# One-row gate matmul widened to 128 rows, and the order of work laid out anew, in a fused attention and gated-MLP kernel

## The chip, the cores and the metric

The kernel runs on one core of a Trainium2 chip. The metric is device time in microseconds (us). Five engines matter here: TensorE (PE in the profile; its weight loads are listed apart as PEld), VectorE (DVE), ScalarE (ACT), GpSimd (POOL), and SyncE (SP), which issues most of the DMAs. Each engine works through its own list of instructions in order, and the engines wait for one another on semaphores.

## The reference

`x` is 2048 tokens of 512 features, in bfloat16. A gate value per token, `g = sigmoid(sum(x * gate_w))`, mixes two branches:

```
g = sigmoid((x * gate_w).sum(-1, keepdims=True))
a = attention(x)             # 32 heads of 16, four segments of 512 tokens
b = ((relu(x @ W_gate)) * (x @ W_up)) @ W_down      # 512 -> 1792 -> 512
return g * a + (1 - g) * b
```

The attention branch takes the tokens in four segments. Inside a segment it is causal softmax attention over 512 tokens per head. Over segments it keeps a memory: `M` and `z` collect the keys (through an elu-like map `phi`) and values of earlier segments, and `num / den` reads them with the queries. The two parts are mixed per head by `sigmoid(beta)`, and a final projection by `wo` follows.

For this case the row `gate_w` matters: 512 numbers in DRAM that every one of the 128 partitions needs as a copy, since the sum over features is taken by VectorE with tokens on partitions.

## The kernel before

**Stages.** All weights are loaded once and stay on the chip. For each segment `s` of 512 tokens there are:

- `proj(s)` (lines 774 to 818): query, key and value projections, 4 x 3 tiles of four 128x512 matmuls (lines 786 and 788).
- `att(s)` (lines 876 to 1023): 18 "visits" of the score matrix. One visit is a block of small matmuls on 32 rows each (line 908, "quad"), which fills four PSUM banks, and one `Exp` by ScalarE over 128x2048 (line 924), which empties them. The next quad writes the same four banks, so it waits for that `Exp`. GpSimd masks the diagonal blocks (line 930). After the visits of a head group comes the product with the values ("pv", line 964, matmuls on 64 rows and 17 columns): 16 in all, followed by VectorE transposes and a scaling.
- `mu(s)` and `nd(s)` (lines 823 to 864): update and read of the memory; `mu` runs as matmuls on 32 columns (line 831), three times in all.
- `ffn(s)` (lines 1028 to 1050): 14 x 2 tiles of four matmuls (line 1038), evacuated by ScalarE or VectorE as relu (lines 1046 and 1047) and by VectorE as a product (line 1049).
- `outp(s)` (lines 1052 to 1093): the output projection and `W_down` into one PSUM bank (lines 1070 and 1077), scaled (lines 1086 and 1087) and stored.

**What sets the order.** The order of instructions on each engine isn't written by hand. Every piece of work is an `Op` with an assumed duration, its reads and writes, and a place in one of several queues per engine with a priority. While the program is built, `Sched.run` (line 486) plays a list scheduler: `ready` (line 308) says when an op could start, `_choose` (line 443) takes the best head of the queues, and `place` (line 364) appends it to the engine's program with the waits that it needs and moves the engine's planned clock on. Equal choices are broken by a random number (`jitter`, line 436) whose seed changes with every 8 us of TensorE's planned time (`knob`, line 428; `WIN`, line 35); the same seed also draws small changes of the priorities. The list of seeds stands at line 546. TensorE's planned clock gets `SWITCH` (line 28) added whenever the op's mode differs from that of the op before (line 392): "f" is a matmul on the full array, "r" a quad, "h" a pv, "c" a `mu`. So a change to one assumed duration, to `SWITCH` or to the seeds changes which op is taken next from that point on, on all engines.

**The gate row.** In the first microseconds ScalarE's queue issues two small DMAs: a 1 KB read into `adT` that is read by nobody (`touch`, line 602) and `gate_w` into row 0 of the tile `oTt` (line 603). The other 127 rows of `oTt` hold whatever they held. SP meanwhile issues the tokens of segment 0 into `hT` (line 604) and the weights. GpSimd builds the identity matrix and masks (lines 646 to 658). TensorE runs five warm-up matmuls, transposes `hT` against the identity (line 683), a second small warm-up (line 699), begins the query projection, and then runs the matmul named `gwx`:

```
lhsT = ones[0:1, 0:128], rhs = oTt[0:1, 0:512]  ->  PSUM bank 2, 128 x 512
```

It has one row of contraction, so each of the 128 output partitions gets one times `gate_w`. ScalarE copies the bank to `gwb` (line 706, `gwc`), and VectorE uses `gwb` in the gate sums (lines 734 and 742). `gwx` may not be planned before 6.4 us (line 705). Later `oTt` serves as scratch for VectorE's transposes (line 992).

Of the kernel before, what the change touches and what calls it, by code (L numbers as in the profile page):

```python
# [11 lines left out]
BF16 = mybir.dt.bfloat16  # L12
# [12 lines left out]
TNN = 4  # L25
STRICT = 6000.0
PE_LAT = 175.0
SWITCH = 100.0
GATE_T = {1: 44000.0, 2: 90000.0, 3: 140000.0}
UNIT_T = 400.0  # L30
NBLK = 36
# [91 lines left out]
class Sched:  # L123
# [240 lines left out]
    def place(self, op, e, start):  # L364
# [26 lines left out]
        if e == "pe":  # L391
            if op.mode != self.mode or start > self.now[e] + 60.0:
                occ += SWITCH
            self.mode = op.mode
# [127 lines left out]
def plan(S, D, F):  # L522
    NT, KT, NF = S // 128, D // 128, F // 128
    return [
        ("xT", [128, KT, XR * 512], BF16), ("wq", [128, KT, 512], BF16), ("wk", [128, KT, 512], BF16), ("wv", [128, KT, 512], BF16),
        ("wo", [128, 4, 512], BF16), ("wg", [128, KT, F], BF16), ("wu", [128, KT, F], BF16), ("wd", [128, NF - SBX, 512], BF16),
        ("qT", [128, QTN, 512], BF16), ("kT", [128, 4, 512], BF16), ("kp", [128, 5, 8, 128], BF16),
        ("phiq", [128, 4, 512], BF16), ("ek", [128, EKN, 512], BF16), ("phik", [128, 4, 512], BF16), ("ttmp", [128, 2, 512], BF16),
        ("vaug", [128, 2, 4, 32, 17], BF16), ("vsh", [128, 4, 32, 17], BF16), ("E", [128, NBLK * 512], BF16),
        ("Tn", [128, TNN, 512], F32), ("adT", [128, 512], BF16), ("oTt", [128, 512], BF16),  # L530
        ("amem", [128, 2, 512], BF16), ("amemT", [128, 4, 512], BF16), ("oT", [128, OTN, 512], BF16),
        ("hT", [128, HTN, 512], BF16), ("rl", [128, 3, 512], BF16), ("osb", [128, 3, 512], BF16),
        ("Mc", [128, 4, 34], F32), ("Mbd16", [128, 4, 136], BF16), ("mumask", [128, 4, 136], F32),
        ("braw", [128, 32], BF16), ("eb", [128, 32], F32), ("romgh", [128, 32], F32), ("epsv", [128, 32], F32),
        ("gexp", [128, NT], F32), ("omg", [128, NT], F32), ("gexpT", [128, NT * 4], F32), ("gwb", [128, 512], BF16),  ("gl", [128, NT], F32),
        ("rden", [128, 64], F32), ("rdg", [128, 64], F32), ("rdm", [128, 128], F32), ("pm8", [128, 8], F32), ("pm", [128, 2], F32), ("ident", [128, 128], BF16),
    ]


def build_kernel(nc, A_x, A_wq, A_wk, A_wv, A_wo, A_beta, W_g, W_u, W_d, gate_w, out):  # L540
    _, S, D = A_x.shape
    F = W_g.shape[1]
    assert D == 512 and S % 512 == 0 and F % 128 == 0
    NSEG, KT, NF, NT = S // 512, D // 128, F // 128, S // 128
    EPS, SCALE = 1e-6, 16 ** -0.5
    sc = Sched(seeds=(140892, 575458, 0, 581332, 635069, 619273, 262375, 763595, 0, 238677, 585783, 19046, 187739, 0, 462444, 519459, 197962, 296149, 243870, 832001, 511906, 535245, 636171, 100007, 0, 121574, 418075, 0, 0, 346384, 0,))
    T = {}
    with contextlib.ExitStack() as stack:
        for name, shape, dt in plan(S, D, F):
            T[name] = stack.enter_context(nc.sbuf_tensor(name, shape, dt))  # L550
        PS = stack.enter_context(nc.psum_tensor("ps", [128, 8, 512], F32))
        for st in sc.streams:
            sc.sem[st] = stack.enter_context(nc.semaphore(f"s_{st}"))
        program(sc, nc, T, PS, A_x, A_wq, A_wk, A_wv, A_wo, A_beta, W_g, W_u, W_d, gate_w, out, NSEG, KT, NF, NT, EPS, SCALE)
        with nc.Block() as block:
            sc.emit(block)
    return sc


def program(sc, nc, T, PS, A_x, A_wq, A_wk, A_wv, A_wo, A_beta, W_g, W_u, W_d, gate_w, out, NSEG, KT, NF, NT, EPS, SCALE):  # L560
    V = type("V", (), T)
    PL = PS[:, 0:4, :]
    PF = PS[:, :, :].rearrange("q b n -> q (b n)")

    def op(eng, fn, occ, **k):
        return sc.add(Op([(eng, fn, occ)], **k))

    def pe(fn, occ, **k):
        k.setdefault("lat", PE_LAT)
        if k.get("role") == "w":  # L570
            k["reads"] = list(k.get("reads", ())) + [f"init{i}" for i in range(4)]
        return op("pe", fn, occ, **k)
# [10 lines left out]
    def pool(fn, occ, **k):  # L583
        return op("pool", fn, occ, **k)

    def dma(eng, fn, nbytes, occ=500.0, **k):
        return op(eng, fn, occ, dma=True, nbytes=nbytes, **k)
# [9 lines left out]
    def load(eng, names, dst, src, nbytes, occ=460.0):  # L597
        (lact if eng == "act" else lsp).append(dma(eng, lambda e, dst=dst, src=src: e.dma_start(dst, src), nbytes, occ=occ, writes=names, name="ld" + names[0]))  # L598
    x0 = A_x[0, 0:512, :].rearrange("(i p) d -> p i d", p=128)
    def touch(n, src):  # L600
        load("act", ["adT"], V.adT[0:16, 32 * n:32 * n + 32], src, 1024)
    touch(0, A_wq[0:16, 0:32])
    load("act", ["oTt"], V.oTt[0:1, :], gate_w.rearrange("(a n) -> a n", a=1), 1024)
    for i in range(4):
        load("sp", [f"hT{i}"], V.hT[:, i, :], x0[:, i, :], 1 << 17)
# [40 lines left out]
    st = []  # L646
# [15 lines left out]
        ds.append(dve(lambda e, b=b: e.memset(PS[:, 4 + b, :], 0.0), 500, writes=[f"init{b}"], name=f"init{b}"))  # L662
    ds.append(dve(lambda e: e.reduce_sum(V.pm[:, :], V.pm8[:, :].rearrange("q (j p) -> q p j", p=2), AX.X), 180, reads=["pm8"], writes=["pm"], name="pm"))
    sc.queue(0, ds)
    sc.queue(1, st)

    def warm(m, n, k, b):
        def fn(e):
            for i in range(m):
                ins = e.matmul(PL[:, b, 0:n], lhsT=nc.const_aps.tensor(1.0, [128, 128], BF16), rhs=nc.const_aps.tensor(1.0, [128, n], BF16), start=True, stop=True)  # L670
            return ins
        return pe(fn, m * n * (0.834 if k == 0 else 0.5), writes=[f"bankL{b}"], name=f"warm{k}")

    xps, xcs = [warm(5, 512, 0, 3)], []
# [26 lines left out]
            ins = e.matmul(A(epw)[:, 0:n], lhsT=nc.const_aps.tensor(1.0, [128, 128], BF16), rhs=nc.const_aps.tensor(1.0, [128, n], BF16), start=True, stop=True)  # L701
        return ins
    xps.append(pe(warm1, 380, name="warm1", ep=epw, role="w"))
    xps.append(pe(lambda e: e.matmul(PL[:, 2, :], lhsT=nc.const_aps.tensor(1.0, [128, 128], BF16)[0:1, :], rhs=V.oTt[0:1, :], start=True, stop=True), 300, reads=["oTt"], writes=["bankL2"], name="gwx"))  # L704
    xps[-1].after = 6400.0
    xcs.append(act(lambda e: e.activation(V.gwb[:], PL[:, 2, :], ACT.Copy), t_act(512), reads=["bankL2"], writes=["gwb"], name="gwc"))
    sc.queue(0, xps)
# [458 lines left out]
def bass_gated_mix__memory_aug_infini_attn__glu_gated_reglu__prompt_kernel(  # L1166
    nc, A_x, A_wq, A_wk, A_wv, A_wo, A_beta, B_x, B_W_gate, B_W_up, B_W_down, gate_w, out
):
    return build_kernel(nc, A_x, A_wq, A_wk, A_wv, A_wo, A_beta, B_W_gate, B_W_up, B_W_down, gate_w, out)
# [28 lines left out]
```

## Time and profile before

| what | value |
|---|---|
| time, median of 3 runs (lowest to highest) | 264.85 us (264.82 to 264.95) |
| the profiled execution's own time | 265.14 us |
| its span, first to last instruction | 263.4 us |
| TensorE busy | 255.4 us, 97% of the span |
| ScalarE busy | 184.9 us, 70% |
| VectorE busy | 181.0 us, 69% |
| GpSimd busy | 129.8 us, 49% |
| DMA engines busy, mean of 16 | 87% from 5.88 to 45 us, 6% to 28% in the stretches after |
| granted TensorE clock | 1.00 over the span |

The profiled execution's time is 1.74 us above its span: that is what lies around the first and the last instruction. A line of the timeline has a start, a length, the engine, the source line, the operation, what it writes and reads, the shape and a count of merged instructions. TensorE's matmuls are pipelined, so the recorded length of one (380 ns for 512 columns) is longer than the distance to the next one's start; the cost of a matmul is read from the distances between starts. A letter q behind an engine's name is its DMA queue or its sequencer.

### The profile page before, as it was taken

The page shows a single profiled execution, that of the slowest core. Times are in us where ns is not written, and L with a number is a line of the kernel's source. Part 1 is how long each engine was busy: PE and PEld are TensorE (multiplying, and loading weights), DVE is VectorE, ACT ScalarE, POOL GpSimd, SP SyncE. Part 2 cuts the span into 40 slices and gives each one's busy share as a digit, 9 for nine tenths or more (in the row PEclk, how much of TensorE's full clock was granted, in tenths as well). Part 3 has the DMA queues.
Part 4 walks back from the last instruction along what each step waited for, and adds up shares of the span by engine and source line. Part 5 has one row for each costly group of instructions (what it writes and reads, how often), then busy time and mean ns, then how long its engine had stood idle before and what let it go on. Part 6 is the DMA issues. An engine that isn't in the chain of part 4 may idle for free.

```text
span 263.4 us, 6630 instructions
## 1 busy us (share of the span) xinstructions
PE 255.4 (97%) x2713; PEld 113.6 (43%) x2748; DVE 181.0 (69%) x355; ACT 184.9 (70%) x159; POOL 129.8 (49%) x295
## 2 busy tenths in 40 slices
PE   8999999999999999999999999999999999999996
PEld 4444444444343544434343444444444444444444
DVE  5788788889788555787877765775873857267610
ACT  4577589976788956877778986978765765767021
POOL 3025646564646354774646366776564443535200
PEclk9999999999999999999999999999999999999999
DMA  6899584024250023210273014110032101100011
GB/s 182 235 383 223 85 270 132 4 41 71 56 115 27 3 65 80 63 41 3 58 138 74 20 42 81 41 25 20 20 80 49 22 0 42 41 2 0 2 40 40
DMA packets 34527, 19.22 MB, mean 73 GB/s; under 512 B 24001, under 2 KB 33986, under 8 KB 34498
## 3 DMA queue, kind: packets, MB, share of 16 engines
q1 hardware_dynamic: 34368, 18.80, 29.4%
q8 instruction: 21, 0.34, 0.5%
q14 instruction: 8, 0.07, 0.1%
q10 hardware_dynamic: 130, 0.01, 0.0%
HBM read 9.75 MB, written 2.11 MB: 45 GB/s over the span
## 4 chain that ended last, share of the span: by engine, by line
PE 94%; DMA 2%; issue 2%; SPq 0%; DVE 0%; DVEq 0%
PE ps L1038 36%; PE ps L1077 19%; PE ps L788 11%; PE ps L908 9%; PE ps L964 7%; PE ps L1070 5%; PE ps L786 5%; DMA phik<-ek 1%; PE ps L851 1%; DMA hT<-in_A_x_dram 1%; PE ps L831 1%; SPq L598 0%; PE ps L683 0%; DVE osb L1086 0%; PE ps L704 0%
## 5 line engine op out<-in xcount | busy, mean ns | idle before, releaser
L930 POOL TENSOR_SCALAR_AFFINE_SELECT E<-E 64x256 bf16<-64x256 bf16 (+1 forms) x256 | 108.9, 437 | 110.1 <-ACT E L924 81.3
L924 ACT ACTIVATE E<-ps 128x2048 bf16<-128x2048 f32 x72 | 135.1, 1876 | 36.4 <-PE ps L908 36.0
L1038 PE MATMUL ps<-xT,wu 128*128 128x512 bf16 x214 | 57.5, 380 | 1.4 <-issue 1.3
L1038 PE MATMUL ps<-xT,wg 128*128 128x512 bf16 x217 | 57.7, 380 | 0.8 <-issue 0.6
L1077 PE MATMUL ps<-wd,hT 128*128 128x512 bf16 (+2 forms) x229 | 52.3, 366 | 1.1 <-issue 1.0
L1049 DVE TENSOR_TENSOR hT<-ps,rl 128x512 bf16<-128x512 f32 x56 | 38.2, 682 | 18.8 <-PE ps L1038 18.4
L974 DVE STREAM_TRANSPOSE Tn<-ps 128x512 f32<-128x512 f32 x32 | 21.2, 695 | 17.8 <-PE ps L964 17.7
L1038 PEld LDWEIGHTS ps<-xT,wg 128*128 128x128 bf16 x224 | 20.6, 98 | 25.9 <-issue 3.5
L1077 PEld LDWEIGHTS ps<-wd,hT 128*128 128x128 bf16 x238 | 21.4, 98 | 23.8 <-issue 2.8
L1038 PEld LDWEIGHTS ps<-xT,wu 128*128 128x128 bf16 x224 | 19.9, 98 | 25.7 <-issue 3.2
L908 PE MATMUL ps<-qT,kp 32*128 32x192 bf16 (+7 forms) x512 | 28.6, 287 | 0.0
L1047 DVE TENSOR_SCALAR rl<-ps 128x512 bf16<-128x512 f32 x31 | 21.3, 688 | 5.0 <-PE ps L1038 4.3
L1046 ACT ACTIVATE rl<-ps 128x512 bf16<-128x512 f32 x25 | 14.9, 598 | 12.8 <-PE ps L1038 12.8
L908 PEld LDWEIGHTS ps<-qT,kp 32*128 32x128 bf16 x512 | 8.2, 92 | 25.8 <-issue 14.4
L964 PE MATMUL ps<-E,vaug 64*17 64x128 bf16 (+7 forms) x512 | 18.7, 283 | 0.0
L964 PE MATMUL ps<-E,vsh 64*17 64x128 bf16 (+7 forms) x512 | 18.3, 283 | 0.0
L1087 ACT ACTIVATE osb<-ps,omg 128x512 bf16<-128x512 f32 (+1 forms) x9 | 6.1, 675 | 15.6 <-PE ps L1070 14.4
L1086 DVE TENSOR_SCALAR osb<-ps,omg 128x512 bf16<-128x512 f32 (+1 forms) x8 | 5.6, 700 | 16.3 <-PE ps L1070 10.1
L1070 PE MATMUL ps<-wo,oT 128*128 128x512 bf16 (+2 forms) x68 | 16.5, 367 | 0.0
L788 PE MATMUL ps<-xT,wk 128*128 128x512 bf16 x62 | 16.2, 380 | 0.2 <-issue 0.2
L788 PE MATMUL ps<-xT,wq 128*128 128x512 bf16 x62 | 15.9, 379 | 0.3 <-issue 0.2
L786 PE MATMUL ps<-wv,xT 128*128 128x512 bf16 x59 | 15.1, 380 | 0.7 <-issue 0.6
(74 smaller groups left out, 232.7 us busy)
## 6 DMA issues: line engine op xcount, KB each, us to landing
vsh<-vaug SPq DMA_DIRECT2D x8, 272.0 KB, 3.9
out_dram<-osb SPq DMA_DIRECT2D x15, 128.0 KB, 1.7
wg<-in_B_W_gate_dram SPq DMA_DIRECT2D x8, 224.0 KB, 5.1
wu<-in_B_W_up_dram SPq DMA_DIRECT2D x8, 224.0 KB, 5.3
wd<-in_B_W_down_dram SPq DMA_DIRECT2D x1, 1792.0 KB, 9.1
osb<-in_A_x_dram SPq DMA_DIRECT2D x12, 128.0 KB, 2.3
hT<-in_A_x_dram SPq DMA_DIRECT2D x4, 128.0 KB, 2.3
wq<-in_A_wq_dram SPq DMA_DIRECT2D x4, 128.0 KB, 2.9
```

The lines of the kernel that those rows point to most:

```text
L786: ins = e.matmul(A(ep)[:, :], lhsT=V.xT[:, kt, tok + col * 128:tok + (col + 1) * 128], rhs=w[:, kt, :], start=(kt == 0), stop=(kt == KT - 1))
L788: ins = e.matmul(A(ep)[:, :], lhsT=w[:, kt, col * 128:(col + 1) * 128], rhs=V.xT[:, kt, tok:tok + 512], start=(kt == 0), stop=(kt == KT - 1))
L908: ins = q.matmul(dst, lhsT=V.kp[r, kslot(s, G), c, :], rhs=V.qT[r, qslot(s, G), q0:q0 + w], start=True, stop=True, tile_position=(32 * jj, ...
L924: acts.append(act(lambda a: a.activation(V.E[:, base * 512:base * 512 + min(2048, 4 * W)], PF[:, 0:min(2048, 4 * W)], ACT.Exp, scale=SCALE ...
L930: pools.append(pool(lambda g, ap=ap, lim=lim, pat=pat: g.affine_select(out=ap, in_=ap, compare_op=ALU.is_ge, fill=0.0, base=lim, pattern=[ ...
L964: ins = q.matmul(A(eps[p])[32 * jj:32 * jj + 17, 64 * (c + u):64 * (c + u + n)], lhsT=v[:, 8 * G + 2 * jj + p, :], rhs=V.E[r, f:f + 64 * n ...
L974: ds.append(dve(lambda e, p=p, ep=eps[p]: e.transpose(V.Tn[:, 2 * (G % (TNN // 2)) + p, :], A(ep)[:, :]), t_dve(512), writes=[f"Tn{2 * (G ...
L1038: ins = e.matmul(A(ep)[:, :], lhsT=w[:, kt, f * 128:(f + 1) * 128], rhs=V.xT[:, kt, c % XR * 512:(c % XR + 1) * 512], start=(kt == 0), sto ...
L1047: ("dve", lambda e, ep=eg, r=r: e.tensor_scalar(V.rl[:, r, :], A(ep)[:, :], 0.0, None, ALU.max), t_dve(512))],
L1049: evs.append(dve(lambda e, ep=eu, r=r, hs=hs: e.tensor_tensor(V.hT[:, hs, :], A(ep)[:, :], V.rl[:, r, :], ALU.mult), t_dve(512), reads=[f" ...
L1070: ins = e.matmul(A(ep)[:, 0:c1 - c0], lhsT=V.oT[:, ot[G], i * 128:(i + 1) * 128], rhs=V.wo[:, G, c0:c1], start=st_ and G == 0, stop=sp_ an ...
L1077: ins = e.matmul(A(ep)[:, 0:c1 - c0], lhsT=V.hT[:, slots[f], i * 128:(i + 1) * 128], rhs=V.wd[:, f, c0:c1], start=st_ and f == f0, stop=sp ...
```

## The change

Four lines change, and one is added:

- `gz`, a new GpSimd instruction, sets all of `oTt` (128 x 512, bfloat16) to zero. It is put second in GpSimd's list, between the two instructions that build the identity. Since it writes `oTt`, the DMA of `gate_w` into row 0 now waits for it.
- `gwx` contracts over all 128 rows of `oTt` with a 128x128 matrix of ones, so 127 of the products are zeros. Its assumed duration falls from 300 to 216 ns.
- `SWITCH` rises from 100 to 104 ns.
- The list of seeds is another one, with 29 entries in place of 31.

The computed values are the same. What each engine does in total is the same but for `gz` and the shape of `gwx`; the order in which the scheduler lays it out is drawn anew.

```diff
-SWITCH = 100.0
+SWITCH = 104.0
...
-    sc = Sched(seeds=(140892, 575458, 0, 581332, 635069, 619273, 262375, 763595, 0, 238677, 585783, 19046, 187739, 0, 462444, 519459, 197962, 296149, 243870, 832001, 511906, 535245, 636171, 100007, 0, 121574, 418075, 0, 0, 346384, 0,))
+    sc = Sched(seeds=(249524, 599739, 0, 545337, 139743, 284348, 57498, 932614, 741284, 496270, 730785, 169184, 0, 723979, 219278, 211335, 0, 499970, 629776, 0, 138415, 940641, 908855, 0, 156145, 0, 475937, 427456, 0,))
...
     touch(0, A_wq[0:16, 0:32])
+    gz = pool(lambda e: e.memset(V.oTt[:, :], 0.0), 250, writes=["oTt"], name="gz")
     load("act", ["oTt"], V.oTt[0:1, :], gate_w.rearrange("(a n) -> a n", a=1), 1024)
...
-    sc.queue(1, st)
+    sc.queue(1, [st[0], gz] + st[1:])
...
-    xps.append(pe(lambda e: e.matmul(PL[:, 2, :], lhsT=nc.const_aps.tensor(1.0, [128, 128], BF16)[0:1, :], rhs=V.oTt[0:1, :], start=True, stop=True), 300, reads=["oTt"], writes=["bankL2"], name="gwx"))
+    xps.append(pe(lambda e: e.matmul(PL[:, 2, :], lhsT=nc.const_aps.tensor(1.0, [128, 128], BF16), rhs=V.oTt[:, :], start=True, stop=True), 216, reads=["oTt"], writes=["bankL2"], name="gwx"))
```

## The prediction, made before the result was known

> **What bounds the kernel now.** I read the page first, then the waits, then TensorE's timeline.
>
> ```profile
> span 263.4 us, 6630 instructions
> PE 255.4 (97%) x2713; PEld 113.6 (43%) x2748; DVE 181.0 (69%) x355; ACT 184.9 (70%) x159; POOL 129.8 (49%) x295
> PE 94%; DMA 2%; issue 2%; SPq 0%; DVE 0%; DVEq 0%
> ```
>
> TensorE is busy for 97% and makes 94% of the chain that ended last; no other engine passes 70%. The question is whether the remaining per cents are idle time that another order could fill. TensorE's own waits:
>
> ```profile
> PE ps L1038 <- issue: 1.9, 12, 0.2
> PE ps L1077 <- issue: 1.0, 6, 0.2
> PE ps L670 <- PEq L1183: 0.8, 1, 0.8
> ```
>
> Apart from the start (0.8) nothing is named but "issue", at most 0.2 us each. The timeline tells what these are:
>
> ```profile
> 24.44 1.03 PE L1038 MATMUL ps<-xT,wu 128*128 128x512 bf16 x4
> 25.40 0.40 PE L908 MATMUL ps<-qT,kp 32*128 32x256 bf16 x8
> 25.73 1.04 PE L1038 MATMUL ps<-xT,wg 128*128 128x512 bf16 x4
> 26.60 0.38 PE L1038 MATMUL ps<-xT,wu 128*128 128x512 bf16 x1
> ```
>
> A full 512-column matmul costs 0.216 us (four in a row between 25.73 and 26.60, 0.87). From 24.44 to 25.40 four take 0.96: entering the quad costs 0.10 more. The quad holds TensorE for 0.33. Where 0.16 of "issue" stands, the next start is one whole 0.216 later, and the groups by line hold 217 and 214 matmuls of L1038 where the program has 448: these are missing records, not idle time. The same holds for the chain's "DMA phik<-ek": in its 3.4 us TensorE's timeline runs on at 0.216 a matmul.
>
> I summed TensorE's work from the first projection (5.88) to the end of the last matmul (260.94), with distances between starts. Wide matmuls: 910 of 512 columns at 0.2158 are 196.4; 18 of 384 at 0.163 and 18 of 128 at 0.056 are 3.9; 48 of the memory read at 0.063 are 3.0. Row- or column-tiled blocks: 72 quads at 0.329 are 23.7, 16 pv at 1.10 are 17.6, 3 mu at 0.59 are 1.8. Entries from full-array matmuls into tiled blocks: I count 74 in the timeline (17 of the 91 blocks follow another tiled block and pay none) at 0.102, 7.5. The gate matmul is 0.41. Together 254.3 of 255.1: at most 0.8 us of the whole stretch can be waiting. TensorE's own work is the bound, with hardly any slack to win.
>
> **The change, part by part.**
>
> *The matmul.*
>
> ```profile
> 5.88 1.02 PE L788 MATMUL ps<-xT,wq 128*128 128x512 bf16 x4
> 6.83 0.38 PE L704 MATMUL ps<-oTt,const-bfloat16-1.0 1*128 1x512 bf16 x1
> 7.15 0.60 PE L788 MATMUL ps<-xT,wq 128*128 128x512 bf16 x2
> ```
>
> The four before it should fill 4 x 0.216 = 0.86 but its start is 0.95 after theirs: 0.09 of entry. Its successor comes 0.32 after it: 0.216 and 0.10 of exit. As a full matmul amid full ones it costs 0.216 like its neighbours, so 0.09 + 0.10 = 0.19 to 0.20 goes. Bounds: 0.20 gained, or nothing if the cost hangs on something other than its one row. I take 0.20, because every full-to-full step around it shows 0.216 and every full-to-tiled one shows the extra.
>
> Here a rule speaks against the change. The Trainium skill's page "TensorE: Matmul & The Clock Gate", section "LDWEIGHTS (loading the stationary operand)", says that a weight load's time goes by its columns and not by the contraction length; its section "Why this matters for your kernels" adds that a single matmul with 32 rows takes as long as one with 128. By that rule the gain is 0 and the time 264.85; by the row above it is 0.20. The trace agrees on the weight load alone, 90 ns with one row against 98 with 128, and not on the distances to the neighbours. The Trainium skill's page "TensorEngine Tiling (Array Packing)", section "Key Properties", has that case: a change of tiling mode drains TensorE.
>
> What is late next if this 0.20 goes: the weights. The four issues of wu end near 12.6 with a median of 5.3 to landing, the last near 17.5; their first reader starts at 18.39. With everything 0.20 sooner 0.7 is left.
>
> *The memset and the later DMA.*
>
> ```profile
> 0.80 0.20 POOL L647 MEMSET ident<- 128x128 bf16 x1 [0.29 <-POOLq L1183]
> 1.08 0.29 POOL L648 TENSOR_SCALAR_AFFINE_SELECT ident<-ident 128x128 bf16<-128x128 bf16 x1
> 1.24 0.54 ACTq L598 DMA_DIRECT2D oTt<-in_gate_w_dram  x1
> 1.81 1.28 ACT L695 ACT_TABLE_LOAD   x1 [1.81 <-issue]
> 2.92 0.37 PEld L683 LDWEIGHTS ps<-ident,hT 128*128 128x128 bf16 x4 [0.70 <-DMA hT<-in_A_x_dram]
> 4.13 1.03 ACT L695 ACTIVATE xT<-ps 128x512 bf16<-128x512 f32 x2 [1.04 <-PE ps L683]
> ```
>
> GpSimd's memset of 512 columns isn't in the trace. From below: 0.20, the memset of 128 columns; from above: four of these, 0.80. Between the 8-column memset (0.10) and the 128-column one (0.20) the slope gives 0.10 + 504 x 0.00083 = 0.52, an estimate from these rows, which I take. Behind it on GpSimd: the identity would be ready near 1.9 (2.2 by the upper bound) in place of 1.37; its reader at 2.92 waits for the tokens' DMA. VectorE's reduction of the mask (3.01) and GpSimd's own next work (15.32) have more room. Cost 0; past 1.5 us of memset it would push the transposes.
>
> The wait stands in ScalarE's queue: the gate DMA goes out near 1.6 (1.9 at most) in place of 1.24, and behind it the table load moves to about 2.2 (2.5) and ends by 3.4 (3.8), before its user at 4.13. SP's queue isn't behind it. The DMA has no landing row; ScalarE's other 1 KB reads land after 1.9 to 4.8, so it is there by about 3.5 (6.7 at the extreme) for a reader at 6.83. Cost 0. If that cover went, the price would be the lateness itself, since the projection stands behind the gate matmul on TensorE.
>
> *The order.* TensorE's instructions are the same set, so the order moves time in two ways only: the number of entries into tiled blocks, and waits. One entry is 0.10. The scheduler takes a pv next to a quad where it can (11 pv run straight into a quad, 3 follow one), so I expect 74 plus or minus 3 entries, 0.3 us, and take 0 for the mean. The four-nanosecond rise of `SWITCH` costs nothing itself; it moves the plan's clock.
>
> Waits can only be added. Their nearest row is the exponential that empties a quad's banks:
>
> ```profile
> 20.23 1.88 ACT L924 ACTIVATE E<-ps 128x2048 bf16<-128x2048 f32 x1 [1.48 <-PE ps L908]
> 22.37 0.40 PE L908 MATMUL ps<-qT,kp 32*128 32x320 bf16 x8
> 22.48 0.60 ACT L1046 ACTIVATE rl<-ps 128x512 bf16<-128x512 f32 x1 [0.37 <-PE ps L1038]
> ```
>
> It ends at 22.11 and the quad starts at 22.37: 0.26 later. Over the quads that distance is 0.26 at the least, in seven of them, and 0.70 in the median, and no quad was late. Bounds of the new waits: 0 as now, and from above these seven each behind one more evacuation of 0.60, 7 x (0.60 - 0.26) = 2.4. I take 0, nearest to the order seen, in which every quad kept the distance. The moved DMA issues sit on SP, which no row shows as a bound.
>
> The tail stays: the last evacuation (0.35) and store follow the last matmul in any order.
>
> **Sum.** Profiled execution: 265.14 (263.4 of span and 1.74 around it) - 0.20 + 0 + 0 = 264.94. It stood 0.29 above the median, so the median goes from 264.85 to 264.65, -0.08%. Within 0.2%, 0.53 us, a measurement of this kernel can hardly tell it from no change.
>
> **Rivals.**
>
> *Fewer entries.* The new draw puts more pv and quads side by side. It is past 0.2% from four entries fewer: -0.20 - 4 x 0.10 = -0.60, 264.25; six give 264.05. For it: 74 entries for 91 blocks leave room, as no pv has a quad on both sides. Against it: 14 of 16 pv already have one quad neighbour, and of idle time there is at most 0.8 us to win.
>
> *Quads behind a late exponential.* Slower than before. The new order puts an evacuation of 0.60 ahead of the exponential on ScalarE, where its quad has the 0.26 only: TensorE, in order, waits 0.34. It decides from three such visits (1.0 less the 0.20 gained is 0.8, over 0.53). With one a segment it is 4 x 0.34 = 1.36: 266.0. For it: the relu sits right beside the exponential on ScalarE (22.48), and seven visits have only the 0.26. Against it: ScalarE is at 70%, and this scheduler kept the distance in every visit.
>
> *The full matmul saves nothing.* The extra at 6.83 would come from what TensorE does there and not from the one row: 264.85. For it: the weight load of one row (90 ns) is as long as one of 128 (98). Against it: the 0.09 before and the 0.10 after stand at every change between full and tiled blocks, and at no full-to-full step.
>
> **Chances.** Forecast (dense, one matmul cheaper) 0.49, its own range 264.3 to 265.2 from three entries either way and one or two short waits; the matmul saving nothing 0.07; both within 0.2%, so 0.56. Fewer entries 0.13, faster. Late exponentials 0.31, slower: the order is new over the whole span and seven visits have little room. The range reaches to the fewer-entries case (264.1) and past the one-a-segment case to five or six visits (5 x 0.34 - 0.20 = 1.5: 266.3), short of the upper bound.
>
> **What the profile after would show.** Line 704 with 128 rows, 0.216 from its predecessor and to its successor. A memset on `oTt` near 1.0 of about 0.5 us and the gate DMA behind it, with the transposes still starting near 2.9. The count of entries into L908 and L964 blocks near 74. TensorE's waits still "issue" only. Distances from exponential to quad still 0.26 or more. The prediction is wrong if quads wait on L924, or another evacuation shows as a releaser of full matmuls, or if a gap opens before 20 us where weights land.

## The result, and the profile after

The changed kernel takes 266.31 us (median of 4 runs, 265.82 to 266.81) against 264.84 us (264.78 to 264.95) for the kernel before: slower by 0.55%, ratio 1.0055, 95% interval 1.0036 to 1.0074. Run once more beside other kernels it took 266.15 us against 264.99, ratio 1.0046 (1.0034 to 1.0058). Its four runs scatter by 1.0 us where those of the kernel before lay within 0.2 us in the same comparison (later 0.5 us in five runs of it, and 0.9 in twenty and more of the kernel before).

The profiled execution took 266.38 us. The page's span, busy times and chain:

```profile
span 264.5 us, 6634 instructions
PE 255.2 (96%) x2713; PEld 113.9 (43%) x2748; DVE 180.0 (68%) x356; ACT 184.3 (70%) x158; POOL 131.1 (50%) x296
PE 91%; DVE 3%; issue 2%; DMA 1%; ACT 1%; POOL 0%; SPq 0%; DVEq 0%
```

TensorE's busy time is 0.2 us less and the span is 1.1 us more, so TensorE now waits. Its waits, by line and releaser (total, times, longest):

```profile
PE ps L832 <- DMA phik<-ek: 0.7, 1, 0.7
PE ps L832 <- issue: 0.6, 1, 0.6
PE ps L1039 <- DVE amem L861: 0.2, 1, 0.2
```

Line 832 is the memory update `mu` (831 before), line 1039 the gate and up projection (1038 before). None of the three stood in the kernel before. (The view's other new rows, 0.2 each, are missing matmul records.) I measured each more exactly, by the distance from the end of one planned op on TensorE to the end of the next (its semaphore updates, which the trace holds in full), less the shortest such distance for the same pair of kinds in any profile:

| from the end of the first 512-column matmul to the last matmul | before | after |
|---|---|---|
| whole stretch | 254.68 us | 256.14 us |
| of it waiting, first `mu` | 0 | 0.80 |
| inside the second `mu` | 0 | 0.72 |
| gate or up tile behind the last memory read of segment 1 | 0.15 | 0.36 |

The three are 1.73 us more. The matmul gives back 0.20 and one entry less 0.10, and the sum, 1.43, is the stretch's 1.46. Ahead of it the changed execution was 0.38 early (the last tokens of the first segment landed at 4.33 in place of 4.83), behind and around it 0.15 longer: 1.46 - 0.38 + 0.15 = 1.23, and the two profiled executions differ by 1.24.

**The three places.** The first `mu` in the changed kernel, from TensorE's timeline, with SP's line of the transposes that it needs:

```profile
33.17 1.03 PE L789 MATMUL ps<-xT,wk 128*128 128x512 bf16 x4
34.93 0.66 PE L832 MATMUL ps<-vaug,phik 128*32 128x34 bf16 x64 [0.73 <-DMA phik<-ek]
...
26.02 6.46 SPq L812 DMA_TRANSPOSE phik<-ek  x4
```

In the kernel before, the same op starts at 42.05, when its last transposed keys have been there since 36.08. The new order puts it at 34.1; they land at 34.88. The scheduler's own plan had them land at 34.1.

The second `mu`, first in the kernel before, then in the changed one:

```profile
89.83 0.40 PE L908 MATMUL ps<-qT,kp 32*128 32x448 bf16 x8
90.15 0.66 PE L831 MATMUL ps<-vaug,phik 128*32 128x34 bf16 x64
90.98 1.24 PE L1077 MATMUL ps<-wd,hT 128*128 128x512 bf16 x5 [0.16 <-issue]
```

```profile
92.72 0.40 PE L909 MATMUL ps<-qT,kp 32*128 32x384 bf16 x8
93.05 0.60 PE L832 MATMUL ps<-vaug,phik 128*32 128x34 bf16 x57
94.24 0.22 PE L832 MATMUL ps<-vaug,phik 128*32 128x34 bf16 x7 [0.59 <-issue]
```

The 64 matmuls of a `mu` have no wait between them, and yet 57 run and then nothing for 0.6. At 94.62 "0.16 <-issue" follows, a missing record as before; the 0.59 is real.

The third, VectorE's lines and the tile behind them on TensorE:

```profile
111.13 0.35 DVE L860 RECIPROCAL rdm<-rdm 128x32 f32<-128x32 f32 x1
111.97 0.75 DVE L861 SCALAR_TENSOR_TENSOR amem<-ps,gexp,rdm 128x512 bf16<-128x512 f32 x1 [0.48 <-DVE rdm L860]
...
112.78 1.04 PE L1039 MATMUL ps<-xT,wg 128*128 128x512 bf16 x4 [0.18 <-DVE amem L861]
```

The memory product (861) frees the PSUM banks that the gate tile takes. It starts 0.49 after the reciprocal ends, though nothing that it needs was open: the DMA that it also waits for, by a second semaphore, had landed at 94.3.

**The matmul and the memset** went as forecast. From TensorE's timeline and the opening lines:

```profile
5.42 1.11 PE L789 MATMUL ps<-xT,wq 128*128 128x512 bf16 x4
6.36 0.38 PE L705 MATMUL ps<-oTt,const-bfloat16-1.0 128*128 128x512 bf16 x1
6.58 0.59 PE L789 MATMUL ps<-xT,wq 128*128 128x512 bf16 x2
```

```profile
0.94 0.53 POOL L603 MEMSET oTt<- 128x512 bf16 x1
1.50 0.47 ACTq L598 DMA_DIRECT2D oTt<-in_gate_w_dram  x1
2.00 1.28 ACT L696 ACT_TABLE_LOAD   x1 [2.00 <-POOL pm L651]
3.05 0.77 PEld L684 LDWEIGHTS ps<-ident,hT 128*128 128x128 bf16 x8 [0.82 <-DMA hT<-in_A_x_dram]
```

### The profile page after: what moved, and what is told of

It reads as the page before. It is cut to its first block, busy times and chain, and to the rows that moved or that the text cites. A ratio compares the mean times of both kernels' runs of the same rounds, so it can differ in the third digit from the quotient of the medians.

```text
span 264.5 us, 6634 instructions
## 1 busy us (share of the span) xinstructions
PE 255.2 (96%) x2713; PEld 113.9 (43%) x2748; DVE 180.0 (68%) x356; ACT 184.3 (70%) x158; POOL 131.1 (50%) x296
## 4 chain that ended last, share of the span: by engine, by line
PE 91%; DVE 3%; issue 2%; DMA 1%; ACT 1%; POOL 0%; SPq 0%; DVEq 0%
PE ps L1039 36%; PE ps L1078 18%; PE ps L789 9%; PE ps L909 8%; PE ps L965 5%; PE ps L787 5%; PE ps L1071 5%; DMA phik<-ek 1%; PE ps L852 1%; PE ps L671 1%; PE ps L832 1%; ACT E L925 1%; PE ps L684 1%; DVE osb L743 1%; DVE qT L798 1%
## 5 line engine op out<-in xcount | busy, mean ns | idle before, releaser
L931 POOL TENSOR_SCALAR_AFFINE_SELECT E<-E 64x256 bf16<-64x256 bf16 (+1 forms) x256 | 110.8, 444 | 112.0 <-ACT E L925 87.2
L1078 PE MATMUL ps<-wd,hT 128*128 128x512 bf16 (+2 forms) x230 | 53.5, 367 | 1.2 <-issue 1.1
L1048 DVE TENSOR_SCALAR rl<-ps 128x512 bf16<-128x512 f32 x32 | 22.0, 688 | 8.1 <-PE ps L1039 7.5
L1047 ACT ACTIVATE rl<-ps 128x512 bf16<-128x512 f32 x24 | 14.3, 597 | 10.4 <-PE ps L1039 10.4
L1088 ACT ACTIVATE osb<-ps,omg 128x512 bf16<-128x512 f32 (+1 forms) x10 | 6.8, 676 | 17.7 <-PE ps L1071 14.0
L965 PEld LDWEIGHTS ps<-E,vaug 64*17 64x17 bf16 x512 | 11.6, 86 | 8.7 <-issue 3.6
```

What stands on the lines that cost most here:

```text
L931: pools.append(pool(lambda g, ap=ap, lim=lim, pat=pat: g.affine_select(out=ap, in_=ap, compare_op=ALU.is_ge, fill=0.0, base=lim, pattern=[ ...
L965: ins = q.matmul(A(eps[p])[32 * jj:32 * jj + 17, 64 * (c + u):64 * (c + u + n)], lhsT=v[:, 8 * G + 2 * jj + p, :], rhs=V.E[r, f:f + 64 * n ...
L1048: ("dve", lambda e, ep=eg, r=r: e.tensor_scalar(V.rl[:, r, :], A(ep)[:, :], 0.0, None, ALU.max), t_dve(512))],
L1078: ins = e.matmul(A(ep)[:, 0:c1 - c0], lhsT=V.hT[:, slots[f], i * 128:(i + 1) * 128], rhs=V.wd[:, f, c0:c1], start=st_ and f == f0, stop=sp ...
```

## The experiments

All keep the order of work on every engine as it is in the kernel that they start from, except for what the edit names, so that one thing changes at a time. Each is compared with the kernel before on the same chip, whose median there was 264.91 (runs 1 to 4), 264.99 (5 to 8) and 265.06 us (9 to 11).

### 1. The matmul alone

The kernel before with the memset and the 128-row matmul; the new op is taken out of the count that seeds the scheduler's random numbers, and the assumed 300 ns stay, so that the order is the old one.

```diff
+    gz = pool(lambda e: e.memset(V.oTt[:, :], 0.0), 250, writes=["oTt"], name="gz")
+    sc.ops.pop()
-    sc.queue(1, st)
+    sc.queue(1, [st[0], gz] + st[1:])
-    ... lhsT=nc.const_aps.tensor(1.0, [128, 128], BF16)[0:1, :], rhs=V.oTt[0:1, :], ...
+    ... lhsT=nc.const_aps.tensor(1.0, [128, 128], BF16), rhs=V.oTt[:, :], ...
```

> The kernel before, its order of work kept exactly on every engine, with only the memset and the 128-row gate matmul. Theory (the matmul gains, the new order loses): 264.84 - 0.20 = 264.64 us, line of the gate matmul 0.216 from both neighbours. Rival (the memset and the later DMA cost at the start): above 264.84, with the transposes or the table load late.

Measured: 264.81 us, ratio 0.9996 (0.9987 to 1.0005). In its trace the matmul has 0.216 to both neighbours, and the stretch from the first projection to the last matmul is 254.50 us, 0.18 less than before. Run again:

> The order before with the 128-row matmul, once more. Theory: 0.20 under the kernel before, ratio 0.9992. Rival: no difference, ratio 1.0000.

264.92 us, ratio 0.9995 (0.9986 to 1.0004). Here the stretch is 254.65, of which 0.17 stands between the ends of the first two projection matmuls. That is no wait: no semaphore stands there, the first three starts are 0.38 and 0.43 apart where 0.216 follows, and the 128-column warm-up matmuls ahead are 0.107 apart where those of the first run are 0.06. TensorE did the first matmuls of this execution at about half its later rate; what decides when it speeds up wasn't tested. So the trace shows the 0.2 and the rival of a lasting cost falls, but the time alone can't tell the gain from nothing: the two runs together read 0.05% less, and the intervals hold both 0 and the 0.08% expected.

### 2. The order alone

The changed kernel with the one-row matmul put back; the memset stays.

```diff
-    ... lhsT=nc.const_aps.tensor(1.0, [128, 128], BF16), rhs=V.oTt[:, :], ...
+    ... lhsT=nc.const_aps.tensor(1.0, [128, 128], BF16)[0:1, :], rhs=V.oTt[0:1, :], ...
```

> The changed kernel, same order on every engine, with the gate matmul back to one row (the memset stays). Theory (the order is to blame): 266.31 + 0.20 = 266.5 us, with the same three waits as in the changed kernel: about 0.8 before the first mu, 0.7 inside the second mu, 0.36 at a gate tile of segment 1. Rival (the wide matmul is to blame for what follows it): back near 264.8.

Measured: 266.67 us, ratio 1.0061 (1.0044 to 1.0078). The three waits are 1.05, 0.72 and 0.35. The order is to blame, and all of the loss is its own.

### 3 and 6. Blocks of instructions

The instruction on which the second `mu` stops is the same in every profile of the changed order with its warm-up as it was: counted over TensorE's weight loads, matmuls and semaphore waits it is number 1986. The trace's queue table has a queue for instructions, q8 with 21 packets of 16 KB, one for about every 256 instructions of TensorE's 5550. For the stretch from 91 to 93.2 us:

```profile
q1 hardware_dynamic: 511, 0.13, 81.0%
q8 instruction: 1, 0.02, 4.5%
```

This packet starts at 91.26 and takes 1.57 us, beside a token read and a transpose. A pv (64 small matmuls, each with a weight load, 128 instructions), a quad (8 and 8, 16) and a `mu` (64 and 64, 128) are 272 instructions in 2.0 us, where a full 512-column matmul with its load spends 0.216 us on two. So I took the gap for TensorE waiting for its next 256 instructions. Two kernels test it by moving the ends of the blocks and nothing else. In the changed kernel the warm-up is cut finer:

```diff
-            for i in range(m):
-                ins = e.matmul(PL[:, b, 0:n], ...
+            for i in range(8 * m):
+                ins = e.matmul(PL[:, b, 0:n // 8], ...
```

> The changed kernel with each of the five warm-up matmuls of 512 columns cut into eight of 64: the same columns, but 70 more instructions (loads and matmuls) at the head of TensorE's list, so that every 256-instruction block of its program ends 70 instructions earlier in the work. Theory (the gap inside the second mu is TensorE waiting for its next block of instructions): the gap of 0.6 inside the second mu goes, 266.31 - 0.7 = 265.6 us. Rival (the gap belongs to the mu itself, its operands or its PSUM bank): the gap stays, 266.3.

Measured: 265.25 us, ratio 1.0008 (0.9997 to 1.0019). The second `mu` runs through:

```profile
92.42 0.40 PE L909 MATMUL ps<-qT,kp 32*128 32x384 bf16 x8
92.75 0.66 PE L832 MATMUL ps<-vaug,phik 128*32 128x34 bf16 x64
93.57 0.38 PE L1078 MATMUL ps<-wd,hT 128*128 128x512 bf16 x1 [0.16 <-issue]
```

The gain, 1.06 us by the medians, is more than the 0.72 of the gap: in this profile the wait ahead of the first `mu` was gone as well, since the keys landed at 34.31 before TensorE came for them, and a new wait of 0.35 for weights of the up projection stood at 19.2.

The other way round, the kernel before is given 46 instructions more ahead, which puts the end of a block where the changed kernel has it:

```diff
-            for i in range(m):
-                ins = e.matmul(PL[:, b, 0:n], ...
+            for k in (8, 8, 8, 2, 2):
+                for i in range(k):
+                    ins = e.matmul(PL[:, b, 0:n // k], ...
```

> The kernel before, same order on every engine, with its warm-up matmuls cut so that TensorE has 46 more instructions ahead of the work (the same columns). One 256-instruction block then ends 10 instructions before the end of the second mu, and the block before it at the start of the pv in front, as in the changed kernel. Theory (a block used up in less than about 3.5 us makes TensorE wait): a gap of about 0.6 appears inside the second mu, 264.9 + 0.6 = 265.5 us. Rival (the gap has to do with the changed kernel's order): no gap, 264.9.

Measured: 266.65 us, ratio 1.0059 (1.0046 to 1.0072): the old order, with not one operation of it moved, is as slow as the new one. The gap is there, after 58 matmuls, and the first instruction behind it is again number 1986:

```profile
89.60 0.40 PE L909 MATMUL ps<-qT,kp 32*128 32x448 bf16 x8
89.93 0.62 PE L832 MATMUL ps<-vaug,phik 128*32 128x34 bf16 x58
91.50 0.22 PE L832 MATMUL ps<-vaug,phik 128*32 128x34 bf16 x6 [0.96 <-issue]
```

It costs 1.09, not 0.6. In the six profiles that have the gap, TensorE goes on 1.24 to 1.42 us after the instruction packet has landed (packet 91.26 + 1.57 = 92.83, go-on 94.24 in the changed kernel; 89.26 + 0.93 = 90.19 and 91.50 here). The size of the gap is what is left of that when TensorE gets there. In the kernel before, the packet lands at 90.92, and the block ends some 35 instructions behind the `mu`, among full matmuls, where there is time for it.

The limit of 3.5 us that was expected isn't shown. Counted back by 256 from number 1986, the block that ends in the gap was used up in 1.84 us, in both orders. Blocks used up in 4.1 us (the kernel before, up to 93.3; run 3, up to 35.1) left no gap, and one used up in 4.5 us (run 8, below) left 0.34.

The Trainium skill's page "Runtime: NRT & Kernel Launch", section "Instruction fetch mechanics", describes this fetch: blocks of 16 KB, 256 instructions, requested while the current one runs, at a cost that it calls mostly hidden. The packets' size agrees with the trace here; the cost is hidden under full matmuls and isn't under this burst, where it is 0.7 to 1.1 us.

### 4. The first mu later

```diff
+LATE = {n: 6600.0 for n in ("mu0", "mum0", "mu16_0")}
...
-    sc.run()
+    sc.replay(SEQ)        # the recorded order, with the ops in LATE 6.6 us of plan later
```

> The changed kernel with the first mu, its accumulation and its four products put 6.6 us of planned time later on their engines, all else in the same order. Theory (the wait for the transposed keys is lost for good): the 0.8 before the first mu goes, 266.31 - 0.8 = 265.5 us. Rival (TensorE is early there and the time comes back as another wait): near 266.3, with a new wait between 35 and 60 us.

Measured: 266.01 us, ratio 1.0027 (1.0014 to 1.0041), against 1.0055 and 1.0046 for the changed kernel: 0.2% to 0.3% less, 0.5 to 0.7 us (the intervals just overlap, so the size is rough). The `mu` starts at 41.42 without a wait and no new one comes up between its old place and 94 (0.32 at the first projection matmuls is the slower start seen in run 11); the other two waits are as they were (0.73 and 0.34). The wait is lost for good, as the theory has it, but its size isn't 0.8 in every run. Over the profiles of the early `mu` it is 0.80 (first profile), 1.05 (run 2), 0.13 (run 5), 0.21 (run 7) and none in runs 3 and 10, with the keys landing between 33.95 and 35.67 us. This is part of the 1 us by which the changed kernel's runs scatter.

> The changed kernel as it is, once more, beside the next three. Theory: 266.3 us, wide spread (about 1 us), since one of its three waits is for DMAs that land by up to 1 us sooner or later; the gap inside the second mu is there again at the same instruction, 0.6 to 0.8. Rival (the waits of the first profile were chance): another set of waits, or a time near 265.

Measured: 266.15 us, with the gap inside the second `mu` at the same instruction (0.82), the wait at the gate tile (0.36) and 0.13 ahead of the first `mu`.

### 7. One semaphore fewer at the memory product

The product waits for the reciprocal and for a DMA. The DMA's wait is put on an earlier op, a gate sum with 3.4 us of idle time behind it.

```diff
+    by = {t.name: t for t in sc.ops}
+    by["gate10"].preds.append((by["aT1_1"], False))
```

> The changed kernel, same order, with VectorE's wait for one DMA (the transpose that reads the memory buffer written next) moved from the memory product to an earlier gate sum, where VectorE idles. Theory (the product starts 0.45 late since it has to wait on two semaphores, and the gate tile behind it on TensorE is late by that): the idle before the product falls from 0.48 to under 0.1, the wait of 0.36 at the gate tile goes, 266.3 - 0.36 = 265.95 us. Rival (the idle belongs to the reciprocal ahead of it): no change, 266.3.

Measured: 265.94 us, ratio 1.0035 (1.0020 to 1.0051), 0.1 to 0.2% under the changed kernel, which its scatter hardly lets one see. The trace is plain (line numbers are those of this file, 1060 is the product):

```profile
110.91 0.35 DVE L1059 RECIPROCAL rdm<-rdm 128x32 f32<-128x32 f32 x1
111.30 0.75 DVE L1060 SCALAR_TENSOR_TENSOR amem<-ps,gexp,rdm 128x512 bf16<-128x512 f32 x1
...
111.35 1.03 PE L1238 MATMUL ps<-xT,wu 128*128 128x512 bf16 x4
112.21 1.03 PE L1238 MATMUL ps<-xT,wg 128*128 128x512 bf16 x4
```

From reciprocal to product 0.04 in place of 0.49, and the gate tile follows at 0.216. So moving the wait takes the pause away. That the second wait is what costs 0.45, as the theory has it, is not borne out: in the changed kernel's own profile the same product, with the same two kinds of wait, starts 0.11 after its reciprocal elsewhere.

```profile
150.32 0.35 DVE L860 RECIPROCAL rdm<-rdm 128x32 f32<-128x32 f32 x1
150.78 0.75 DVE L861 SCALAR_TENSOR_TENSOR amem<-ps,gexp,rdm 128x512 bf16<-128x512 f32 x1
```

In the order before, the pause stands ahead of another op, the output scaling, and its memory product behind it has none:

```profile
109.92 0.75 DVE L1086 TENSOR_SCALAR osb<-ps,omg 128x512 bf16<-128x512 f32 x1 [0.68 <-PE ps L908]
110.59 0.74 DVE L860 SCALAR_TENSOR_TENSOR amem<-ps,gexp,rdm 128x512 bf16<-128x512 f32 x1
```

What the two have in common is their place. Counted over VectorE's instructions and separate semaphore waits, the op behind the pause is number 192 in all nine profiles that have one (0.40 to 0.43 behind the last thing that it waited for), in both orders, and no other op of VectorE behind the first 20 is held up for over 0.15 by nothing that the trace names. 0.7 to 0.9 us after it starts, a packet follows in q14, a second queue for instructions (110.60 before, 112.72 in the changed kernel). In the four profiles without the pause (runs 7 to 10) that packet comes earlier, at 106.2 to 107.4. This looks like the end of a block of VectorE's own instructions, moved out of the way together with the wait; no run moved that end alone, so it is argued and not shown.

### 8 and 10. Together

Run 8 is the changed kernel with the finer warm-up of run 3, the first `mu` later as in run 4, and the earlier wait of run 7:

```diff
+            for i in range(8 * m):
+                ins = e.matmul(PL[:, b, 0:n // 8], ...
+    by["gate10"].preds.append((by["aT1_1"], False))
+    sc.replay(SEQ)        # with the ops in LATE 6.6 us of plan later
```

> The changed kernel with all three at once: warm-up cut (70 instructions more ahead), first mu 6.6 us later, wait moved to the gate sum. Theory (the three waits are the whole loss): 266.3 - 0.7 - 0.8 - 0.36 = 264.45 us, and no wait of TensorE over 0.1 after the first projection. Rival (other waits come up behind them): 265 or more.

Measured: 265.30 us, ratio 1.0012 (0.9999 to 1.0025). None of the three waits is left, but 0.34 has come up elsewhere, 0.25 inside a pv and 0.09 behind it (by the 1.18 and 0.26 of the other pv and the quads behind them in that profile):

```profile
45.41 0.20 PE L1164 MATMUL ps<-E,vaug 64*17 64x64 bf16 x3
45.77 0.18 PE L1164 MATMUL ps<-E,vaug 64*17 64x64 bf16 x1 [0.16 <-issue]
45.88 0.40 PE L1108 MATMUL ps<-qT,kp 32*128 32x448 bf16 x8
```

It stands where a block ends again (at instruction 961, four blocks ahead of number 1986 to within one), and 1.20 us after a packet landed: cutting the warm-up and moving the first `mu` together put the end of an earlier block at the end of a pv. So the rival was right: another wait came up. Run 10 leaves the first `mu` where the changed kernel has it:

```diff
-    sc.replay(SEQ)
+    sc.run()
```

> The changed order with the warm-up cut (70 instructions) and VectorE's wait moved, but the first mu left early. Theory: 266.2 - 0.7 - 0.36 = 265.1 us, plus or minus what the wait for the transposed keys takes in a run (0 to 1). Rival (the cut of the warm-up alone made the 1.0 of the third run, by way of the keys as well): 264.9 or less.

Measured: 264.96 us, ratio 0.9997 (0.9988 to 1.0006), stretch 254.30 with no wait over 0.11: no end of a block falls badly, and the keys were there in time again. The new order without its three waits is as good as the old one, 0.2 us of the stretch being the matmul. The time doesn't separate the theory (265.1, by what the keys take) from the rival (264.9 or less). Why the keys came early enough in both kernels with the cut warm-up, and late in the others, wasn't settled: the DMA rings carried the same transfers, but an instruction packet that fell at 32 to 33 us in the others fell at 31.0 us in runs 3 and 10.

### 9. A version that beats both

The old order, the 128-row matmul, and the second waits of the output scaling and of the memory product moved to an earlier gate sum:

```diff
+    by["gate9"].preds += [(by["aT1_1"], False), (by["st1"], False)]
```

> The order before, with the 128-row matmul, and VectorE's two DMA waits ahead of the output scaling and the memory product near 109 moved to an earlier gate sum. Theory: the matmul gives 0.20, and the last wait of that order (0.15 at a tile of the up projection near 111) goes: 264.9 - 0.35 = 264.55 us. Rival (runs of this kernel scatter by more than that and the start decides): not to be told from the kernel before.

Measured: 264.61 us against 265.06, ratio 0.9982 (0.9973 to 0.9991). TensorE's stretch is 254.36, 0.32 below the kernel before, with no wait over 0.11 in it. It is 0.18% faster, and the trace names 0.20 of it as the matmul's and 0.15 as the wait's at the up projection's tile; of all kernels run it is the only one whose interval lies wholly below 1.

## Why the prediction was wrong

The forecast was 264.65 us and the range 264.1 to 266.3; the time was 266.31, slower, which had a chance of 0.31. Step by step:

- *What bounds the kernel* was right: TensorE's own work, with 0.8 us at most of waiting. Every loss found is a wait of TensorE, and nothing else moved its stretch in the changed kernel but the matmul and the one entry.
- *The matmul* was right: 0.09 and 0.10 are gone, both distances are 0.216. The rule of the Trainium skill's page "TensorE: Matmul & The Clock Gate", section "Why this matters for your kernels", by which the contraction length doesn't count does not hold for one narrow matmul between full ones; the 0.09 and 0.10 fit the drain named on the Trainium skill's page "TensorEngine Tiling (Array Packing)", section "Key Properties", though the runs show its cost and not the drain itself. "What is late next", the up projection's weights, came late in run 3, by 0.35, and not in either run of the matmul alone.
- *The memset and the later DMA* were right, nearly to the digit: 0.53 for the estimate of 0.52, the DMA at 1.50 (1.6 forecast), the table load done at 3.28 (3.4), the transposes at 3.05 still behind the tokens' DMA, cost 0.
- *The entries* were right: 73 in the new timeline, 74 plus or minus 3 forecast.
- *The waits* are the step that failed: "I take 0, nearest to the order seen". Run 2 shows 1.6 us for the order alone (ratio 1.0061). The bounds looked at one kind of wait, the quad behind its exponential, and that one did not come: the distance is 0.21 at the least in the new order, 0.26 or more in all but one, and 0.70 in the median as before. Three others did. "The moved DMA issues sit on SP, which no row shows as a bound" passed over the keys' transposes, which in the order before had 6 us to spare and in the new one less than none. VectorE's pause was in the old trace too, where it cost TensorE 0.15 that I took for nothing. And the block of instructions was in no row that I read, though the page lists its queue and the burst of 272 instructions in 2.0 us stood in the timeline.
- *The late-exponential rival* had the right sign and by its size (266.0) nearly the right time, for a wrong reason: that was luck, and it isn't borne out. *Fewer entries* gave one, not four. *The full matmul saves nothing* fell in the trace.

## What to carry to other kernels

When an engine is dense, a new order can only add waits beyond the count of its transitions, so each class of wait in the old order should be asked for its smallest margin: not just the commonest one, but the DMAs that had time to spare only because their reader stood late. A change of the order, or of the mere number of instructions ahead, also moves the ends of the instruction blocks; where a burst of small matmuls used up a block in 1.8 us, that alone was worth 0.7 to 1.1 us, and cutting a warm-up differently undid it. When an edit takes a pause away, look whether the same op pauses elsewhere in the profile before naming the cause: moving a semaphore wait helped here, though an op with the same two waits went on without the pause elsewhere.

## What the runs showed of the hardware that was not expected

- TensorE stops inside an op that has no waits when it reaches the end of a block of 256 instructions before the next is there. In six profiles, of two orders, it goes on 1.24 to 1.42 us after the 16 KB packet has landed. Adding 46 instructions to an untouched order made it 1.7 us slower by the medians (266.65 against 264.99), 1.09 of it in this gap in the profiled execution; the rest wasn't placed.
- VectorE paused for 0.40 to 0.43 us ahead of its instruction number 192 in nine profiles of two orders, with all that it waited for there in time; the same kind of op with two waits went on 0.11 us after the one before it elsewhere. Why it pauses there is argued above and not shown.
- A single one-row matmul between full ones costs 0.19 to 0.20 us over its 0.216, the same 0.09 to 0.10 a side as the entry into a block of 32-row matmuls.
